# Four Q/K products moved across blocks, the sums of x in another order, and W1's last tiles split beside the MLP

## The chip, the cores and the metric

One Trainium2 chip, one of its cores. The metric is the device time of one execution in microseconds (us). Each kernel is run several times and the median counts.

## The reference, cut to what matters

The input x has 2048 tokens of 1024 features. It is normalised (xn), goes through multi-head attention with 32 heads of 32 features (s), and beside it through a two-layer MLP with the Mish activation and a SiLU behind it (g); the result is x + s * g.

```python
xn = _layernorm(x)
qkv = xn @ wqkv                                   # 1024 -> 3 x 1024, 32 heads of 32
scores = einsum("bhqd,bhkd->bhqk", q, k) * 32 ** -0.5
s = (softmax(scores) @ v) @ wo
h = xn @ w1 + b1                                  # 1024 -> 3584
act = h * tanh(softplus(h))                       # Mish
g = silu(act @ w2)                                # 3584 -> 1024
out = x + s * g
```

## The kernel before, in words

All matmuls are done with numbers split into two parts, a rounded high part (copied on ScalarE, ACT) and the remainder, the low part (a subtraction on VectorE, DVE, or on GpSimd, POOL). A full product is three matmuls: high by high, high by low, low by high (`THREE`). Split x lies in eight tiles `xc[c][half]`, for four chunks c of 512 tokens and two halves of the features. The program runs in four stages.

**Normalisation and V.** x is normalised, transposed and split, chunk by chunk, while V's first half is computed; a second pass of 16 groups (`v_group(1, t)`, the loop over i from 0 to 15) computes V's second half, 24 matmuls a group. During this second pass DVE computes sums and differences of the chunks of x (`t_half`, 16 calls, one behind each group), which the next stage needs: for the token pair of chunks 0 and 1 they go to DRAM (`ts`), for the pair 2 and 3 they overwrite chunks in place that have had their last use. One of them, `ts[4]`, goes through DRAM and comes back as `xr`. Beside this W1's first tiles are split on POOL and stored (`w1_early`, `W1_V` of the 28 tiles), and split x is stored for the MLP (`x_store`). At group 9 the raw weights of block 0 are loaded, at 11 POOL forms their sums, at 12 and 13 the first four weight pieces are split.

**Q and K.** Sixteen blocks q, of 128 columns each of Q and of K for one token pair (blocks 0 to 7 for chunks 2 and 3, 8 to 15 for chunks 0 and 1). A block computes a 2 x 2 block product with seven instead of eight smaller products, as Strassen and Winograd do; the products are named `A11, S2, A12, S3, S1, A22, S4` = 0 to 6, and a product is 12 matmuls (`product`). It needs a piece of weights (`piece`: a copy on ACT, a subtraction), sums of raw weights (`w_sum`), and one of seven tiles of x (`X`). Between the products ACT and DVE evacuate (`e0`, `e1`, `e3`, `out_`), and pieces are prepared two products ahead. Before block 8 five of the tiles of x are reloaded with those of the other token pair: `x_load` is called behind products 0 to 4 of block 7 (`NEXT`), and each of its four slices waits on SyncE's queue (SP) until PE has read the slice that it overwrites. SP's queue works in order; raw weights (`q_load`), the stores and loads of W1 half tiles (`presplit`, up to three a block, split on POOL) and `x_load` share it. From block 11 on, score matmuls of head 0 (`s_mm`) run between the products; at block 9 the tiles for them are filled with constants (`stacks`, `hl_`, `pad2`).

**The planned part.** Scores, exponentials, the product with V, the MLP's two layers and the start of the output projection run interleaved. A planner (`Plan`) writes the order of every engine out when the program is built, from costs and due times; `LEAN`, a string of digits with one for each 21 us of planned time, tilts its choices. POOL adds the exponentials up (`z`). In the first of four chunks W2 is loaded raw through one buffer (`w2r`), split (ACT, POOL) and stored; `w2` is a ring of five tiles, and W1's tiles come split from DRAM (`load_w1`).

**The end.** The rest of the output projection, SiLU, the product and the sum with x.

Of the kernel before, what the change touches and what calls it, by code (L numbers as in the profile page):

```python
# [18 lines left out]
P = 128  # L19
# [7 lines left out]
W1_V = 8  # L27
# [23 lines left out]
LEAN = ("13000510047567756073468724860620770704718277635355470747314774488"  # L51
        "67603848577224744706616776073777870776675418742527505766070872000")
# [176 lines left out]
def body(ctx: ExitStack, tc: tile.TileContext, x, wqkv, wo, w1, b1, w2, out):  # L229
# [319 lines left out]

    def piece(n, eng):  # L550
        q, i = divmod(n, 7)
# [3 lines left out]
        src = {A11: raws[q][0][:, :HK], A12: raws[q][0][:, HK:], A22: raws[q][1][:, HK:]}.get(i)  # L555
        if src is None:
            src = sums[q][i]
# [11 lines left out]
    def t_half(p, k, half):  # L569
# [3 lines left out]
        def whole(out_, c, kk):  # L573
            u = xc[c][kk][:, :, k]
            nc.vector.tensor_tensor(out_, u[:, 0].bitcast(F32), u[:, 1].bitcast(F32), ALU.add)

        def less(out_, a, b):
            nc.vector.tensor_tensor(out_, a, b, ALU.subtract)

        def split(i, src, home):  # L580
            dst = staged(f"ts{p}_{k}_{i}") if home is None else home[:, :, k]
            copy(dst[:, 0], src)
            low(nc.vector, dst[:, 1], src, dst[:, 0])
            if home is None:
                move(ts[i][:, :, k], dst)
# [9 lines left out]
        else:  # L595
            less(t[2], t[2], t[0])
            whole(t[3], c0, 1)
            less(t[3], t[2], t[3])
            split(1, t[2], None if p else xc[3][0])
            split(3 if p else 4, t[3], None)  # L600

    for i, t in enumerate([4, 5, 6, 7, 12, 13, 14, 15, 0, 1, 2, 3, 8, 9, 10, 11]):
        v_group(1, t)()
        if i % 2 == 0 and i < 10:
            w1_early()
        if i in (0, 2, 4, 6, 9, 11, 13):
            x_store()
        t_half(1 if i < 8 else 0, i % 8 // 2, i % 2)
        if i == 9:
            q_load(0, [vp.tile([P, KT, P], F32, tag="x", name=f"raw{half}", bufs=XB) for half in range(2)])  # L610
        if i == 11:
            s12 = vp.tile([P, 2, HK, P], F32, tag="x", name="s12", bufs=XB)
            s3 = vp.tile([P, 2, HK, P], F32, tag="x", name="s3", bufs=XB)
            w_sum(nc.gpsimd, 0, S1, s12[:, 0])
            w_sum(nc.gpsimd, 0, S2, s12[:, 1])
            w_sum(nc.gpsimd, 0, S3, s3[:, 0])
        if i in (12, 13):
            for n in (2 * (i - 12), 2 * (i - 12) + 1):
                piece(n, nc.gpsimd)
# [18 lines left out]
    def stacks(pool_, i):  # L638
# [3 lines left out]
        if i == 0:  # L642
            nc.gpsimd.memset(qst[i][96:P, :].bitcast(F32), 0.0)
            move(zeros, qst[i][96:P, :])
            nc.vector.memset(kst[i][96:P, :].bitcast(F32), 0.0)
# [66 lines left out]
    jobs = iter([(f, half) for f in range(W1_V, FT) for half in range(2)])  # L712
# [18 lines left out]
    def s_tile(which):  # L731
        return sp.tile([P, HK, P], F32, tag=f"ws{which}", name=f"ws{which}")

    def x_load(dst, src):
        for k in range(HK):
# [26 lines left out]
    def product(q, i, bank_, e):  # L762
        c0, c1 = PAIRS[q // KT]
        w, xx = pieces.pop(7 * q + i), X[q // KT][i]
# [3 lines left out]
        n = 0  # L768
        for k in range(HK):
            for a, b in THREE:  # L770
                nc.tensor.matmul(ps, w[:, a, k], xx[:, b, k], start=n == 0 and i in (0, 1, 4), stop=n == 3 * HK - 1,  # L771
                                 skip_group_check=i not in (0, 1, 4))
                n += 1

        def after():
            if i in (0, 1, 3):
                e[i] = sp.tile([P, 512], F32, tag=f"e{i}", name=f"e{q}_{i}")
# [22 lines left out]
    for q in range(NQ):  # L800
        bank_, e = {}, {}
        for i in range(7):
            n = 7 * q + i
            after = product(q, i, bank_, e)
            if n >= 2 and n % 2 == 0:
# [692 lines left out]
```

## Time and profile before

| | us |
|---|---|
| median of 3 runs | 3402.02 |
| lowest and highest | 3395.75, 3402.33 |
| the profiled execution | 3399.99 |
| its span in the profile | 3398.2 |
| busy: PE (matmul) | 3355.3 |
| busy: DVE, POOL, ACT | 2540.1, 2516.8, 2037.3 |

The span is what the profiler saw from the first to the last instruction; the profiled execution's own time is 1.8 us longer. Busy time is the sum over an engine's instructions. A row of the timeline gives start, duration, engine, line of the program, operation, output and inputs, and in brackets the idle time of the engine just before it and what released it. PE's matmuls are pipelined, so a row's duration holds some overlap with the next. SPq and ACTq are the queues on which SP and ACT issue DMAs.

### The profile page before, as it was taken

The page shows a single profiled execution, that of the slowest core. Times are in us where ns is not written, and L with a number is a line of the kernel's source. Part 1 is how long each engine was busy: PE and PEld are TensorE (multiplying, and loading weights), DVE is VectorE, ACT ScalarE, POOL GpSimd, SP SyncE. Part 2 cuts the span into 40 slices and gives each one's busy share as a digit, 9 for nine tenths or more (in the row PEclk, how much of TensorE's full clock was granted, in tenths as well). Part 3 has the DMA queues.
Part 4 walks back from the last instruction along what each step waited for, and adds up shares of the span by engine and source line. Part 5 has one row for each costly group of instructions (what it writes and reads, how often), then busy time and mean ns, then how long its engine had stood idle before and what let it go on. Part 6 is the DMA issues. An engine that isn't in the chain of part 4 may idle for free.

```text
span 3398.2 us, 45889 instructions
## 1 busy us (share of the span) xinstructions
PE 3355.3 (99%) x16867; PEld 2461.8 (72%) x16867; DVE 2540.1 (75%) x4020; ACT 2037.3 (60%) x3272; POOL 2516.8 (74%) x759
## 2 busy tenths in 40 slices
PE   8989899999999999999999999999999999999999
PEld 7868677677777767777677777777777767777787
DVE  6566588878788877888778877888888777886542
ACT  5333234666776667666666676666676666666621
POOL 1236454999999999888888798887888888888800
PEclk9999999999999999999999999999999999999999
DMA  6989987444344454343334533343445443333382
GB/s 206 316 303 300 305 260 237 142 128 150 119 146 136 135 165 148 101 125 106 119 102 123 185 114 114 110 127 98 128 116 182 126 118 119 106 118 118 132 302 86
DMA packets 308115, 532.75 MB, mean 157 GB/s; under 512 B 88794, under 2 KB 153306, under 8 KB 285658
## 3 DMA queue, kind: packets, MB, share of 16 engines
q1 hardware_dynamic: 288180, 488.15, 46.0%
q10 hardware_dynamic: 19712, 41.69, 3.4%
q8 instruction: 133, 2.18, 0.3%
q14 instruction: 90, 0.74, 0.1%
HBM read 379.55 MB, written 149.16 MB: 156 GB/s over the span
## 4 chain that ended last, share of the span: by engine, by line
PE 91%; DMA 3%; DVE 3%; POOL 1%; ACT 1%; issue 1%; SPq 1%; ACTq 0%; POOLq 0%; DVEq 0%
PE y L1240 18%; PE h L1150 18%; PE t L969 14%; PE s L887 13%; PE pv L1016 13%; PE op L1339 5%; PE v L351 3%; PE q_y L771 2%; PE q_x L771 2%; PE q_z L771 2%; PE zp L1042 1%; DMA w1e<-in_B_w_dram 1%; PE pt L420 0%; DMA praw<-in_B_w_dram 0%; DVE mx L677 0%
## 5 line engine op out<-in xcount | busy, mean ns | idle before, releaser
L998 POOL TENSOR_TENSOR z<-z,p 128x2048 f32<-128x2048 f32 x448 | 2067.3, 4615 | 150.0 <-ACT p L282 126.1
L282 ACT ACTIVATE p<-t,zero 128x512 f32<-128x512 f32 x2048 | 1374.5, 689 | 544.7 <-PE t L969 526.8
L893 DVE TENSOR_REDUCE mx<-s 128x1 f32<-128x512 f32 x1984 | 1325.6, 687 | 401.7 <-PE s L887 393.6
L1240 PE MATMUL y<-w,act 128*128 128x512 f32 x2688 | 928.1, 391 | 0.1
L969 PE MATMUL t<-qstack,kstack 128*128 128x512 f32 x2048 | 798.7, 392 | 1.0 <-DMA qstack<-mt 1.0
L887 PE MATMUL s<-kstack,qstack 128*128 128x512 f32 x1984 | 774.2, 393 | 3.0 <-DVE mx L893 1.5
L1150 PE MATMUL h<-xr,w 128*128 128x512 f32 x2016 | 700.3, 390 | 0.0
L1240 PEld LDWEIGHTS y<-w,act 128*128 128x128 f32 x2688 | 503.6, 188 | 112.7 <-issue 5.0
L969 PEld LDWEIGHTS t<-qstack,kstack 128*128 128x128 f32 x2048 | 383.3, 188 | 109.7 <-issue 20.9
L1016 PE MATMUL pv<-p,v 128*32 128x512 f32 x4096 | 459.3, 594 | 0.0
L887 PEld LDWEIGHTS s<-kstack,qstack 128*128 128x128 f32 x1984 | 369.9, 188 | 121.7 <-issue 23.5
L1150 PEld LDWEIGHTS h<-xr,w 128*128 128x128 f32 x2016 | 378.2, 188 | 81.3 <-issue 2.5
L1262 DVE TENSOR_TENSOR yacc<-yacc,y 128x512 f32<-128x512 f32 x416 | 283.0, 681 | 63.3 <-PE y L1240 62.4
L1016 PEld LDWEIGHTS pv<-p,v 128*32 128x32 f32 x4096 | 123.4, 110 | 283.1 <-issue 282.1
L998 POOL TENSOR_TENSOR z<-p,p 128x2048 f32<-128x2048 f32 x32 | 148.1, 4627 | 183.8 <-PE zp L1042 112.9
L1150 PE MATMUL h<-xc,w 128*128 128x512 f32 x672 | 228.2, 391 | 0.3 <-ACT p L282 0.3
L351 PE MATMUL v<-vw,xc 128*128 128x512 f32 x768 | 179.9, 393 | 0.1
L351 PEld LDWEIGHTS v<-vw,xc 128*128 128x128 f32 x768 | 143.4, 189 | 30.3 <-ACT xc L285 0.6
L1150 PEld LDWEIGHTS h<-xc,w 128*128 128x128 f32 x672 | 125.9, 188 | 26.6 <-ACT p L282 0.7
L771 PE MATMUL q_y<-xc,wq 128*128 128x512 f32 x480 | 120.5, 399 | 13.8 <-DVE e L760 5.2
L285 ACT ACTIVATE act<-h 128x512 fp32r<-128x512 f32 x112 | 66.6, 595 | 88.9 <-DVE h L1199 87.9
L771 PEld LDWEIGHTS q_y<-xc,wq 128*128 128x128 f32 x480 | 91.1, 192 | 36.7 <-DVE e L760 5.7
(139 smaller groups left out, 2947.9 us busy)
## 6 DMA issues: line engine op xcount, KB each, us to landing
w<-w1s SPq DMA_DIRECT2D x112, 1024.0 KB
w<-w2s SPq DMA_DIRECT2D x168, 512.0 KB
w2s<-w SPq DMA_DIRECT2D x56, 512.0 KB
qstack<-qs SPq DMA_DIRECT2D x96, 256.0 KB
kstack<-ks SPq DMA_DIRECT2D x96, 256.0 KB
w1s<-pw SPq DMA_DIRECT2D x40, 512.0 KB
qs<-qst ACTq DMA_DIRECT2D x32, 512.0 KB
ks<-qst ACTq DMA_DIRECT2D x32, 512.0 KB
```

The source lines that it names most:

```text
L282: nc.scalar.activation(out_, in_, fn, bias=zero if bias is None else bias, scale=scale)
L351: nc.tensor.matmul(ps, xc[t // 4][k // HK][:, a, k % HK, (t % 4) * P:(t % 4 + 1) * P], vw[i, k // 2][:, b, k % 2], start=n == 0, stop=n == ...
L771: nc.tensor.matmul(ps, w[:, a, k], xx[:, b, k], start=n == 0 and i in (0, 1, 4), stop=n == 3 * HK - 1, skip_group_check=i not in (0, 1, 4))
L887: nc.tensor.matmul(sp_, qst[h % 3][:, qt * P:(qt + 1) * P], kst[h % 3][:, kc * 512:(kc + 1) * 512], start=True, stop=True)
L893: nc.vector.reduce_max(tiles["mx"][:, qt, kc:kc + 1], tiles[qt, kc], axis=AX.X)
L969: nc.tensor.matmul(tp, kst[h % 3][:, kt * P:(kt + 1) * P], qst[h % 3][:, c * 512:(c + 1) * 512], start=True, stop=True)
L998: nc.gpsimd.tensor_tensor(zs[h], pts[T - 1] if kt == 1 else zs[h], pts[T], ALU.add)
L1016: nc.tensor.matmul(pv[h][c * DH:(c + 1) * DH, :], vt[h][:, k, :], pts[T - kt + k][:, c * 512:(c + 1) * 512], start=k == 0, stop=k == NT - 1)
L1150: nc.tensor.matmul(t["h"], w1t[n][:, a, k], xts_[c][k // HK][:, b, k % HK], start=i == 0, stop=i == 3 * KT - 1)
L1240: nc.tensor.matmul(t["y"], acts[n][:, p, s * P:(s + 1) * P], w2t[m_][:, q], start=j == 0 and i == 0, stop=j == YB - 1 and i == 2)
L1262: nc.vector.tensor_tensor(ya, ya, t["y"], ALU.add)
L1339: nc.tensor.matmul(ps[t, dh], ohl[t // 4, k][:, a, s * P:(s + 1) * P], wt[k][:, b, r], start=k == 0 and i == 0, stop=k == KT - 1 and i == 2)
```

## The change

- Products (7, 0) and (7, 2) move into block 6, behind (6, 2) and (6, 3); (8, 0) and (8, 2) into block 7, behind (7, 4) and (7, 5) (`SEQ`). The tiles of x that they release are reloaded in another assignment (`X[1]`, `NEXT`). `e0` gets a second buffer.
- The half sums of x are taken from a list, two of them behind groups 8, 10 and 12, so that all are issued by group 12. In each second half three instructions move from DVE to POOL. The raw weights of block 0 are loaded at group 5 into tiles that live on (`held`), their four sums formed at group 8, the first pieces split at groups 13 and 14 with DVE; the second load and DVE's sums at the entry to Q/K go.
- W1: 4 instead of 8 tiles are split early, 17 instead of 20 as half tiles in the Q/K stage (not in blocks 6 to 8 instead of not in 7 and 8), and the last 7 as 14 half-tile jobs in the planned part, one with each tile of h from the third on (`w1_job`), through the `w2` ring and the `w2r` buffer, split on ACT and DVE.
- W2: a raw load takes its `w2` tile at once, and every second low part moves from POOL to DVE.
- At block 9 three constant fills move from DVE to POOL; from block 11 on every second piece's low part moves from DVE to POOL; the weight sums, `q_load` and the fills are issued with the pieces instead of behind the products.
- The digits of `LEAN` are others.

```diff
-W1_V = 8
+W1_V, W1_Q, W1_JOB = 4, 21, 2
...
+    EARLY = {(6, 2): [(7, 0)], (6, 3): [(7, 2)], (7, 4): [(8, 0)], (7, 5): [(8, 2)]}
+    MOVED = [x for v in EARLY.values() for x in v]
+    SEQ = [x for q in range(NQ) for i in range(7) if (q, i) not in MOVED for x in [(q, i)] + EARLY.get((q, i), [])]
+    held = {w: big.tile([P, HK, P], F32, tag=f"ws{w}", name=f"ws{w}") for w in (S1, S3, S4)}
...
         else:
+            whole(t[3], c0, 1, nc.gpsimd)
             less(t[2], t[2], t[0])
-            whole(t[3], c0, 1)
-            less(t[3], t[2], t[3])
+            less(t[3], t[2], t[3], nc.gpsimd)
             split(1, t[2], None if p else xc[3][0])
-            split(3 if p else 4, t[3], None)
+            split(3 if p else 4, t[3], None, nc.gpsimd)
+    halves = [(p, k, half) for p in (1, 0) for k in range(HK) for half in range(2)]
     for i, t in enumerate([4, 5, 6, 7, 12, 13, 14, 15, 0, 1, 2, 3, 8, 9, 10, 11]):
         v_group(1, t)()
-        if i % 2 == 0 and i < 10:
+        if i == 0:
             w1_early()
...
-        t_half(1 if i < 8 else 0, i % 8 // 2, i % 2)
-        if i == 9:
+        if i == 5:
             q_load(0, [vp.tile([P, KT, P], F32, tag="x", name=f"raw{half}", bufs=XB) for half in range(2)])
-        if i == 11:
...
+            nc.sync.dma_start(held[S3], wqkv[HK * P:, D:D + P].rearrange("(k p) f -> p k f", p=P))
+        if i == 8:
+            s23 = vp.tile([P, 2, HK, P], F32, tag="x", name="s23", bufs=XB)
+            for which, to in ((S1, held[S1]), (S2, s23[:, 0]), (S3, s23[:, 1]), (S4, held[S4])):
+                w_sum(nc.gpsimd, 0, which, to)
+        for _ in range(2 if i in (8, 10, 12) else 1):
+            if halves:
+                t_half(*halves.pop(0))
+        if i in (13, 14):
+            for n in (2 * (i - 13), 2 * (i - 13) + 1):
+                piece(n, nc.vector)
...
-            nc.vector.memset(kst[i][96:P, :].bitcast(F32), 0.0)
+            nc.gpsimd.memset(kst[i][96:P, :].bitcast(F32), 0.0)
             nc.vector.memset(kst[i][96:98, :].bitcast(F32), 1.0)
...
-         [xc[0][0], xc[2][0], xc[0][1], xc[3][0], xc[2][1], xc[1][0], xc[1][1]])
+         [xc[0][0], xc[2][0], xc[0][1], xc[2][1], xc[3][0], xc[1][0], xc[1][1]])
-    NEXT = {0: (X[1][1], ts[1]), 1: (X[1][3], ts[2]), 2: (X[1][4], ts[0]), 3: (X[1][5], ts[3]),
+    NEXT = {0: (X[1][1], ts[1]), 2: (X[1][3], ts[2]), 1: (X[1][4], ts[0]), 3: (X[1][5], ts[3]),
...
-    q_load(0, ring_of(0))
     q_load(1, ring_of(1))
     x_load(xr, ts[4])
-    sums[0] = {}
-    for which in (S1, S2, S4):
-        w_sum(nc.vector, 0, which, s_tile(which))
...
+    for n, (q, i) in enumerate(SEQ):
+        after = product(n)
+        for m in (n + 2, n + 3) if n >= 2 and n % 2 == 0 else ():
+            piece(m, nc.vector if q < 11 or m % 2 else nc.gpsimd)
...
+        if i in (0, 2, 5) and not 5 < q < 9:
+            presplit()
...
+        own = op("SP", 0.1, emit=raw, take=["w2", "w2r"], bytes_=P * 512 * 4)
+        a = op("ACT", 0.6, need=[own], emit=lambda at: copy(t["w"][:, 0], t["raw"]))
+        a = op("DVE", 0.73, need=[a], emit=lambda at: low(nc.vector, t["w"][:, 1], t["raw"], t["w"][:, 0]), give=["w2r"])
+        w1_kept.setdefault(f, []).append(op("SP", 0.1, need=[a], emit=keep, give=[("w2", own)], bytes_=P * 1024 * 4))
...
-        a = op("SP", 0.1, emit=raw, need=need, take=["w2r"], bytes_=P * 512 * 4)
-        w2_took[m] = a = op("ACT", 0.6, need=[a], emit=high, take=["w2"])
+        w2_took[m] = a = op("SP", 0.1, emit=raw, need=need, take=["w2", "w2r"], bytes_=P * 512 * 4)
+        a = op("ACT", 0.6, need=[a], emit=high)
...
+        w2_ops[m] = a = op("DVE" if m % 2 else "POOL", 0.73 if m % 2 else 1.3, need=[a], emit=rest, give=["w2r"],
+                           key=None if m % 2 else -1)
...
+            if 0 <= n - W1_JOB < 2 * (FT - W1_Q):
+                w1_job(W1_Q + (n - W1_JOB) // 2, (n - W1_JOB) % 2)
```

More of the change, by code (lines that the diff above doesn't have):

```diff
@@ L554, in piece @@
         w = pieces[n] = pieces["tile"][:, :, n % 2 * HK:n % 2 * HK + HK]
[L555 to L557 removed]
+        if i == A22:
+            src = raws[q][1][:, HK:] if q else held[S3]
+        else:
+            src = raws[q][0][:, :HK] if i == A11 else raws[q][0][:, HK:] if i == A12 else sums[q][i]
         copy(w[:, 0], src, scale=-1.0 if i == A22 else 1.0)
@@ L710, in load_w1 @@
         move(w1t[n], w1s[n % FT])
-    jobs = iter([(f, half) for f in range(W1_V, FT) for half in range(2)])
+    jobs = iter([(f, half) for f in range(W1_V, W1_Q) for half in range(2)])
     def presplit():
@@ L731, in s_tile @@
     def s_tile(which):
-        return sp.tile([P, HK, P], F32, tag=f"ws{which}", name=f"ws{which}")
+        return (sp if which == S2 else big).tile([P, HK, P], F32, tag=f"ws{which}", name=f"ws{which}")
     def x_load(dst, src):
@@ L760, in plus, with product @@
         nc.vector.tensor_tensor(out_, a, b, ALU.add)
-    def product(q, i, bank_, e):
+    banks_, es = {}, {}
+    def product(n):
+        q, i = SEQ[n]
+        bank_, e = banks_.setdefault(q, {}), es.setdefault(q, {})
         c0, c1 = PAIRS[q // KT]
-        w, xx = pieces.pop(7 * q + i), X[q // KT][i]
+        w, xx = pieces.pop(n), X[q // KT][i]
         if i in (0, 1, 4):
```

112 lines of the change are left out of this document (53 added, 59 removed).

## The prediction

> **What bounds the kernel now.** I read the page first, then the windows, then the timeline where the windows show a hole, then who was waited for.
>
> ```profile
> span 3398.2 us, 45889 instructions
> PE 3355.3 (99%) x16867; PEld 2461.8 (72%) x16867; DVE 2540.1 (75%) x4020; ACT 2037.3 (60%) x3272; POOL 2516.8 (74%) x759
> ```
>
> TensorE (PE) is the bound, and the change removes none of its matmuls. Only time in which PE stands or runs slowly can be won or lost. The windows say where that is (span, then busy time and count of each engine, granted clock, DMA share, GB/s):
>
> ```profile
> 200.80:242.90 42.10, 30.70 (x109) 23.55 (x107) 24.09 (x31) 10.30 (x19) 14.82 (x12) 0.84 0.81 257
> 242.90:353.20 110.30, 110.10 (x484) 90.82 (x485) 74.29 (x95) 39.50 (x71) 75.56 (x61) 1.00 0.92 300
> 353.20:401.40 48.20, 40.81 (x163) 30.52 (x161) 22.46 (x32) 13.59 (x24) 10.94 (x8) 0.90 1.01 338
> 401.40:446.10 44.70, 42.70 (x171) 34.74 (x172) 28.40 (x36) 13.56 (x24) 25.03 (x19) 0.91 0.85 260
> 446.10:562.40 116.30, 113.79 (x489) 90.64 (x488) 96.67 (x149) 33.17 (x63) 51.26 (x44) 1.00 0.78 248
> 562.40:1310.00 747.60, 742.83 (x3826) 526.75 (x3825) 600.82 (x958) 521.73 (x849) 685.17 (x199) 1.00 0.47 146
> 1310.00:3219.10 1909.10, 1909.10 (x9970) 1362.30 (x9969) 1499.98 (x2360) 1280.34 (x2018) 1610.45 (x372) 1.00 0.40 122
> ```
>
> The second row is the Q/K stage undisturbed: 110.30 us for 484 matmuls, 0.228 each, so 2.73 us for a product of 12. The planned part (last two rows) has 4.8 us of idle PE in 2657, so hardly anything to win. The holes are in rows one, three and four, where the clock falls too.
>
> **Part A, the entry to Q/K (sums of x, weights of block 0).** PE in the timeline:
>
> ```profile
> 200.81 2.88 PE L771 MATMUL q_x<-xc,wq 128*128 128x512 f32 x12
> ...
> 210.48 0.49 PE L771 MATMUL q_y<-xc,wq 128*128 128x512 f32 x1 [4.75 <-ACT xc L285]
> ...
> 212.76 5.28 PE L771 MATMUL q_x<-xc,wq 128*128 128x512 f32 x12
> 223.07 5.34 PE L771 MATMUL q_y<-xc,wq 128*128 128x512 f32 x12 [5.02 <-DVE e L760]
> 228.25 2.92 PE L771 MATMUL q_z<-xc,wq 128*128 128x512 f32 x12
> 231.01 2.88 PE L771 MATMUL q_y<-xr,wq 128*128 128x512 f32 x12
> ...
> 242.97 3.04 PE L771 MATMUL q_x<-xc,wq 128*128 128x512 f32 x12 [0.92 <-ACT e L285]
> ```
>
> Four products take 228.25 - 200.81 = 27.4 us instead of 10.9, so 16.5 are lost, and 1.0 more at 242.97: 17.5. What they waited for, in the timelines of POOL, ACT, DVE and SP:
>
> ```profile
> 194.89 1.29 POOL L548 TENSOR_TENSOR s<-raw 128x512 f32<-128x512 f32 x1 [28.23 <-DMA raw<-in_A_wqkv_dram]
> 197.58 0.63 ACT L285 ACTIVATE wq<-s 128x512 fp32r<-128x512 f32 x1 [3.68 <-POOL s L548]
> 220.27 0.69 DVE L548 TENSOR_TENSOR ws<-raw 128x512 f32<-128x512 f32 x1 [7.73 <-DMA raw<-in_A_wqkv_dram]
> 213.17 5.09 SPq L540 DMA_DIRECT2D raw<-in_A_wqkv_dram  x4
> 218.31 3.69 SPq L289 DMA_DIRECT2D xr<-ts  x4
> ```
>
> First wait: ACT stands in order behind weight pieces whose sums came late, and the last sums of x stand behind it. Second: DVE stands for block 0's raw weights, loaded a second time at 213.17, with the evacuation that PE needs behind it. The change issues raw weights four V groups earlier and only once, keeps the sums in tiles that live on, and finishes all 16 half sums at group 12 of 0 to 15, three groups (about 16 us) before the entry. Both waits go. Next late is xr, needed at product 5, 200.8 + 13.7 = 214.5. SP is free for it after the last V store, about 202, then two raw issues (5.09 / 4 each) and four of xr (3.69): done about 208.5. Today xr was there at most 12.7 us after its first issue (218.31 to 231.01, no wait); from 205 that is 217.7, 3 us late at worst. Four early W1 tiles leave this stretch, whose SP and POOL they occupied; they return as jobs in the planned part (below).
>
> Against it: a third of the half sums' DVE work moves to POOL, and the two disturb each other:
>
> ```profile
> 200.54 1.78 DVE L293 TENSOR_TENSOR ts<-turned,ts 128x512 fp32r<-128x512 f32 x1
> 211.84 0.69 DVE L293 TENSOR_TENSOR ts<-turned,ts 128x512 fp32r<-128x512 f32 x1
> 200.03 1.75 POOL L293 TENSOR_TENSOR wq<-s,wq 128x512 fp32r<-128x512 f32 x1
> ```
>
> The same DVE instruction takes 1.78 beside POOL and 0.69 alone. 24 instructions of up to 1.75 on POOL are 42 us of overlap at most; at a loss of 1.09 in 1.78 that holds DVE up 26 us over the whole stage, where it does 24 x 0.69 = 17 less: 9 us net at worst, inside the 16 of lead. The Trainium skill, "GPSIMD Engine Reference", section 1 (Specifications), says GpSimd's SBUF interfaces are shared with VectorE, with contention for DVE instructions with two SBUF inputs; the three rows agree. By that rule moving work to POOL gains nothing for DVE, and A would be worth what the lead leaves: this is a rival below. I leave 2 of the 17.5 (bounds 0 and 9): **-15.5**.
>
> **Part B, the change of token pairs.** Today five chunk halves are reloaded as products of blocks 7 and 8 release them:
>
> ```profile
> 352.30 2.88 PE L771 MATMUL q_x<-xc,wq 128*128 128x512 f32 x12
> ...
> 385.63 0.93 PE L771 MATMUL q_y<-xc,wq 128*128 128x512 f32 x3
> 387.85 0.98 PE L771 MATMUL q_y<-xc,wq 128*128 128x512 f32 x3 [1.29 <-DMA xc<-ts]
> ...
> 396.21 2.90 PE L771 MATMUL q_z<-xc,wq 128*128 128x512 f32 x6 [3.48 <-DMA xc<-xs]
> ...
> 406.86 2.90 PE L771 MATMUL q_y<-xc,wq 128*128 128x512 f32 x12
> ```
>
> 385.63 to 406.86 is 21.2 us for three products of 2.73, so 13.0 are lost: some 11 of late data and 2 of slow clock. The DMA view of 353.2 to 401.4:
>
> ```profile
> DMA packets 10929, 16.28 MB, mean 338 GB/s; under 512 B 494, under 2 KB 3820, under 8 KB 10927
> ...
> xc<-ts SPq DMA_DIRECT2D x16, 512.0 KB
> ```
>
> Twenty slices of 512 KB are 10.5 MB of the 16.3, and the DMA share was 1.01: bandwidth, not order, is the limit. With (7,0) after (6,2), the first release comes 4 products or 10.9 us earlier; the last use, (8,6), keeps its place. More must now pass: a second pair of raw tiles (1.05 MB) and two more Q/K stores (1.05), less one W1 store (0.5): 1.6 MB, 4.7 us at 338. The data is 11 - 10.9 + 4.7 = about 4.8 late; the W1 half-tile jobs dropped in block 6 take some off. I leave 4.5 (bounds 0 and 9): **-8.5**. Moving the products adds no work: a second buffer for e0 only.
>
> **Part C, the fills at block 9.**
>
> ```profile
> 411.13 1.81 POOL L643 MEMSET qstack<- 32x2048 f32 x1
> 417.64 1.76 DVE L645 MEMSET kstack<- 32x2048 f32 x1 [0.48 <-issue]
> 422.65 4.58 PE L771 MATMUL q_z<-xc,wq 128*128 128x512 f32 x12 [2.00 <-DVE e L760]
> ```
>
> Two such fills hold DVE, and PE loses 2.00 and 4.58 - 2.88 = 1.7 of slow clock: 3.7. One fill goes to POOL, but the other (of ones, over it) then waits on DVE for POOL, which has two sums and the 1.81 fill ahead; behind it in DVE's queue stand a piece and (9,3)'s evacuation, for which (9,5) waits. By my count that arrives between 0 and 4 us late; I take 1: **-2.7**. On the slow clock the Trainium skill, "TensorE: Matmul & The Clock Gate", part 1, says it halves after an idle window of about 3.4 us. Here a wait of 2.00 was enough, so the row decides; by the page C would be worth 1.7 less.
>
> **Part D, blocks 11 to 15.** Every second piece's low part goes from DVE (busy 96.67 of 116.30) to POOL (51.26). PE idles 2.5 there. Bounds -2.5 to +3 (pieces stuck behind POOL's jobs); I take **-0.7**.
>
> **Part E, the planned part.** New leanings reorder the same matmuls: the orders show 96 changes into column mode in both. W1's last 7 tiles come as 14 half jobs through W2's single raw buffer; half of W2's low parts move from POOL to DVE. SP's issues into that buffer, and W1's loads:
>
> ```profile
> 721.66 0.43 SPq L1105 DMA_DIRECT2D w2r<-in_B_w_dram  x1
> 735.63 0.55 SPq L1105 DMA_DIRECT2D w2r<-in_B_w_dram  x1
> 741.95 0.56 SPq L1105 DMA_DIRECT2D w2r<-in_B_w_dram  x1
> 756.77 0.55 SPq L1105 DMA_DIRECT2D w2r<-in_B_w_dram  x1
> L289 SPq DMA_DIRECT2D w<-w1s x112: 319/344/779, 557.1 to 3172.0; - x112
> ```
>
> A use of the buffer takes 14.0, 6.3 and 14.8 us (long behind POOL's z sums); a tile of h has (3172.0 - 557.1) / 111 = 23.6. New per tile: one half behind POOL 14.4, one on DVE 6.3, one W1 job 6.3: 27, over 23.6 for 14 tiles, but before and behind them there is slack of 2.9 a tile. Other streams cover it, as the 4.8 us of idle PE suggest. Bounds -3 and +9; I take **+0.6**.
>
> **Sum:** -15.5 - 8.5 - 2.7 - 0.7 + 0.6 = -26.8. The profiled execution took 3399.99 (3398.2 and 1.8 around it), 2.0 under the median of 3402.02: 3373.2 + 2.0 = **3375**.
>
> **Rivals.** (1) Bandwidth keeps B: the loads start earlier but finish where they did, since blocks 6 and 7 already fill the queues (0.92 of share in row two). B gains 1.5 instead of 8.5: 3382. (2) DVE and POOL slow each other so that the last sums of x still miss the entry: A keeps 9: 3382. (3) Slower: the raw buffer. 14 tiles x 3.4 us = 48 us of W2 lateness, if the five W2 tiles ahead and the attention streams don't cover it: 3375 + 48 = 3423. It decides from some 27 us uncovered on; against it, today's chain refills the buffer without a pause (741.95, 756.77) and PE does not wait for it. (4) The new order of the planned part loses what Q/K wins: 3402.
>
> **Chances:** forecast 0.62, (1) 0.14, (2) 0.11, (3) 0.06, (4) 0.07. A measurement can tell about 0.2%, 6.8 us. Faster: 0.62 + 0.14 + 0.11 less 0.01 for overlap of (1), (2) and bad bounds: 0.86; same 0.07; slower 0.07. Range: best bounds of A, B and C alone give 3375 - 2 - 4.5 - 1 - 3 = 3364, all to the good 3360; (1) and (2) together, with D's bound, give 3393. So 3361 to 3394.
>
> **What would show it.** Right: PE's first eight products after the V stage without a gap over 1 us and at clock 1.00; the loads xc<-ts starting 11 us earlier relative to block 8; raw weights loaded once. Wrong: a wait of q_y on xr, of q_z on xc<-xs as long as 3.48, a DVE fill waiting on POOL at block 9, waits of y on w2, or a planned part over 2836 us.

## The result, and the profile after

| | before | after |
|---|---|---|
| median of 4 runs, us | 3401.35 | 3456.51 |
| lowest and highest | 3395.75, 3402.33 | 3451.74, 3461.32 |
| the profiled execution, its span | 3399.99, 3398.2 | 3455.92, 3454.1 |
| first score of the planned part starts (end of Q/K) | 562.36 | 550.08 |
| from there to the end of the span | 2835.8 | 2904.0 |

The changed kernel is slower by 1.7%: the ratio to before is 1.0166, interval 1.0148 to 1.0184. The spans differ by 55.9 us. Q/K ended 12.3 us earlier and the rest took 68.2 us longer.

From the page of after:

```profile
span 3454.1 us, 45962 instructions
PE 3375.7 (98%) x16867; PEld 2469.0 (71%) x16867; DVE 2634.9 (76%) x4023; ACT 2049.4 (59%) x3286; POOL 2510.2 (73%) x740
```

From its windows, with the columns of the windows shown of before:

```profile
550.10:1310.00 759.90, 713.40 (x3544) 495.41 (x3546) 659.20 (x929) 493.49 (x798) 615.01 (x160) 0.98 0.48 147
1310.00:3219.10 1909.10, 1909.10 (x9969) 1362.94 (x9961) 1504.87 (x2385) 1281.47 (x2023) 1604.87 (x372) 1.00 0.41 123
```

The same number of matmuls, but the first stretch of the planned part got through 3544 in 760 us, where before got through 3826 in 748. From there to 3219 us hardly anything differs. In the first stretch DVE is busy 58 us more. PE stands 46.5 us in it (759.90 less 713.40), where before it stood 4.8. That is 42 of the 68 us; some 26 are left for matmuls that took longer, 201 ns of busy PE each on average against 194 (713.40 / 3544 and 742.83 / 3826), at a granted clock of 0.98 instead of 1.00. Whom PE waited for in that stretch of after (total, times, longest; the first three rows):

```profile
PE t L976 <- DVE mx L900: 14.6, 9, 3.4
PE s L894 <- DVE mx L900: 12.9, 8, 2.9
PE s L894 <- DVE yacc L1290: 3.7, 2, 2.3
```

Two rows more for the maxima, of 3.7 and 2.8, make it 34.0 us for them. Before, the largest row of this list was 1.5 us in all (`PE s`, for the same maxima). Where DVE's time went, from the groups of instructions (count, busy us, mean ns of one):

```profile
L900 DVE TENSOR_REDUCE mx<-s 128x1 f32<-128x512 f32 x556 | 366.4, 684 | 63.3 <-PE s L894 61.1
L293 DVE TENSOR_TENSOR w<-w2r,w 128x512 fp32r<-128x512 f32 x28 | 64.5, 2304 | 7.7 <-ACT w L285 7.6
L293 DVE TENSOR_TENSOR w1w<-w1r,w1w 128x512 fp32r<-128x512 f32 x14 | 43.8, 3128 | 5.5 <-ACT w1w L285 5.5
L1227 DVE TENSOR_TENSOR h<-h,r 128x512 f32<-128x512 f32 x28 | 19.4, 693 | 0.3
```

The second and third rows are the 42 low parts that the change put on DVE. They take 2.30 and 3.13 us, though the same subtraction takes 0.69 where POOL is idle. The fourth row is a multiplication of the same size, one of whose inputs (`h`) lies in PSUM: 0.693. The 42 are the only DVE instructions of this size in the stretch with both inputs in SBUF. Of the 108 us of the 42, 42 x 0.69 = 29 are their own work; 79 are not. What a long one waits for is seen in the timelines of DVE, POOL and PE side by side:

```profile
611.04 2.99 DVE L293 TENSOR_TENSOR w1w<-w1r,w1w 128x512 fp32r<-128x512 f32 x1
613.96 6.55 DVE L900 TENSOR_REDUCE mx<-s 128x1 f32<-128x512 f32 x10
608.88 4.60 POOL L1005 TENSOR_TENSOR z<-z,p 128x2048 f32<-128x2048 f32 x1
613.55 4.93 POOL L1005 TENSOR_TENSOR z<-z,p 128x2048 f32<-128x2048 f32 x1
614.69 0.50 PE L976 MATMUL t<-qstack,kstack 128*128 128x512 f32 x1 [1.57 <-DVE mx L900]
```

The low part is issued at 611.04, while POOL is in the middle of a sum of 4.60 us. It ends at 614.03, which is 0.55 after the end of POOL's sum (608.88 + 4.60 = 613.48), about its own length of 0.69. Ten maxima stand behind it, and PE waits 1.57 for one of them. The Trainium skill, "SBUF — State Buffer", section "Who interferes with whom", has this rule: a DVE instruction with two SBUF inputs and a GpSimd instruction that reads SBUF exclude each other for the whole instruction. The trace agrees with it here, 2.99 against 0.69.

In the Q/K stage, PE's timeline of after at the sites of A (first three rows), B (two), C (two) and D:

```profile
204.55 4.70 PE L784 MATMUL q_x<-xc,wq 128*128 128x512 f32 x12 [3.96 <-ACT wq L285]
223.36 0.97 PE L784 MATMUL q_y<-xr,wq 128*128 128x512 f32 x3 [1.18 <-DMA xr<-ts]
237.78 2.88 PE L784 MATMUL q_z<-xc,wq 128*128 128x512 f32 x12
350.33 2.97 PE L784 MATMUL q_y<-xc,wq 128*128 128x512 f32 x12 [0.88 <-DVE e L769]
373.12 5.46 PE L784 MATMUL q_y<-xc,wq 128*128 128x512 f32 x12 [3.50 <-issue]
402.42 4.58 PE L784 MATMUL q_y<-xc,wq 128*128 128x512 f32 x12 [1.91 <-DVE e L769]
409.58 2.88 PE L784 MATMUL q_x<-xc,wq 128*128 128x512 f32 x12
435.19 0.70 PE L682 MATMUL s<-kstack,qstack 128*128 128x512 f32 x2 [3.69 <-DMA w1s<-pw]
```

The fifth row names no releaser for its 3.50; DVE's evacuation of that bank ran from 372.33 to 373.01, right ahead of it. The third row is product 4 of block 1, which before started at 248.94: A won 11.2. The seventh is the start of block 10, before at 427.07: 17.5 won so far, so B and C together 6.3. By the first score of the planned part 12.3 were left: blocks 10 to 15 lost 5.2. Six of the runs below have the same V and Q/K stages; in their profiled executions Q/K ended at 551.58 to 555.42, and in one with those of before at 559.92. So these executions put what Q/K won at 4.5 to 12.3 us, and differences of a few us in its end say little.

### The profile page after: what moved, and what is told of

The parts are those of the page before. It is cut to its first block, busy times and chain, and to the rows that moved or that the text cites. A ratio compares the mean times of both kernels' runs of the same rounds, so it can differ in the third digit from the quotient of the medians.

```text
span 3454.1 us, 45962 instructions
## 1 busy us (share of the span) xinstructions
PE 3375.7 (98%) x16867; PEld 2469.0 (71%) x16867; DVE 2634.9 (76%) x4023; ACT 2049.4 (59%) x3286; POOL 2510.2 (73%) x740
## 4 chain that ended last, share of the span: by engine, by line
PE 85%; DVE 8%; DMA 3%; ACT 2%; issue 1%; POOL 0%; SPq 0%; ACTq 0%; DVEq 0%; POOLq 0%
PE y L1268 17%; PE h L1178 16%; PE t L976 13%; PE s L894 12%; PE pv L1023 12%; PE op L1367 5%; PE v L351 3%; PE q_y L784 2%; DVE w L293 2%; DVE mx L900 2%; PE q_x L784 1%; PE q_z L784 1%; DVE w1w L293 1%; PE zp L1049 1%; ACT p L282 1%
## 5 line engine op out<-in xcount | busy, mean ns | idle before, releaser
L894 PE MATMUL s<-kstack,qstack 128*128 128x512 f32 x1984 | 779.3, 396 | 17.5 <-DVE mx L900 12.9
L1178 PE MATMUL h<-xc,w 128*128 128x512 f32 x672 | 238.5, 402 | 3.1 <-DVE mx L900 2.8
```

The lines of the kernel that those rows point to most:

```text
L894: nc.tensor.matmul(sp_, qst[h % 3][:, qt * P:(qt + 1) * P], kst[h % 3][:, kc * 512:(kc + 1) * 512], start=True, stop=True)
L1178: nc.tensor.matmul(t["h"], w1t[n][:, a, k], xts_[c][k // HK][:, b, k % HK], start=i == 0, stop=i == 3 * KT - 1)
```

## The experiments

All times are medians; each ratio is to runs of the kernel before on the same chip, with its interval. "Planned part" is the span less the start of the first score behind Q/K.

### What costs 68 us in the planned part

**The low parts taken off DVE and POOL.** Theory H is that held DVE instructions cost the time; the rival O is that the W1 jobs, the raw buffer and the order do.

```diff
-a = op("DVE", 0.73, ..., emit=lambda at: low(nc.vector, t["w"][:, 1], t["raw"], t["w"][:, 0]), ...)
+a = op("DVE", 0.73, ..., emit=lambda at: copy(t["w"][:, 1], t["w"][:, 0].bitcast(F32), scale=0.001), ...)
...   (and the same for the odd tiles of W2)
```

> The changed kernel with its plan kept; the 42 low parts in question are neither on DVE nor on POOL but written by ACT as a thousandth of the high part (this part of the result is left out). DVE then has no instruction with two SBUF inputs in the planned part. Theory H (the held DVE instructions cost the 68 us): PE's waits for DVE's maxima go from some 31 us to under 6, the planned part from 2904 to 2838-2860 us, the time to 3390-3412. Rival O (the 14 W1 jobs, the raw buffer and the order cost the time by themselves): the planned part stays above 2880, the time above 3432.

Measured: 3388.84, ratio 0.9970 (0.9957 to 0.9983). Q/K ends at 552.42 and the planned part takes 2832.5. Whom PE waited for from there to 1310 (the largest two rows):

```profile
PE t L976 <- ACT p L282: 0.6, 2, 0.4
PE t L976 <- DMA qstack<-mt: 0.5, 2, 0.3
```

The window:

```profile
552.40:1310.00 757.60, 755.41 (x3907) 534.48 (x3906) 613.14 (x969) 558.88 (x917) 662.27 (x173) 1.00 0.53 161
```

The jobs, the digits and every other instruction's place are those of after, and the whole loss is gone (2904.0 less 2832.5 is 71.5), with no wait for the maxima left on the list. The kernel leaves the true low parts out. Its raw buffer also comes free sooner, since for these 42 only ACT's first copy reads it; the next run has that too and keeps 50 of the 68 us, so the buffer isn't the cause. O falls. The plain work of 29 us leaves DVE too in this run, but it is less than half of the 71.5; the next three runs change the holding in other ways.

**One SBUF input instead of two.** The 42 become a multiplication of the high part by a constant, still on DVE (`nc.vector.tensor_scalar(w[:, 1], w[:, 0], 0.001, ...)`); the true low parts are left out here too.

> The changed kernel with its plan and the place of every instruction kept. The 42 low parts that it put on DVE in the planned part (14 of W1, 28 of W2) are no longer a subtraction of two SBUF tiles but a thousandth of the high part, an instruction with one SBUF input: this part of the result is left out. Theory H (a DVE instruction with two SBUF inputs is held until POOL lets go, and the maxima behind it stand): these 42 take 0.7 us or less each instead of 2.3 and 3.1 mean, PE's waits for DVE's maxima fall from some 31 us to under 8, and the planned part from 2904 us to 2845-2870, the time to 3398-3422. Rival O (the order itself, the 14 W1 jobs and the raw buffer cost the time): the 42 become short, the planned part stays at 2885 or more, the time at 3437 or more. Rival P (any DVE instruction is held beside POOL, whatever its inputs): the 42 stay at 2 us or more each, and the time within 8 us of 3456.

Measured: 3443.98, ratio 1.0130 (1.0113 to 1.0146); planned part 2886.2. The two groups, in answers on their lines (shortest, median and longest ns):

```profile
L1138 DVE TENSOR_SCALAR w<-w x28: 408/1984/4687, 574.8 to 1281.4; 128x512 fp32r<-128x512 f32 x28
L1109 DVE TENSOR_SCALAR w1w<-w1w x14: 427/2948/4450, 612.9 to 967.9; 128x512 fp32r<-128x512 f32 x14
```

H in my wording, held because of two inputs, missed: with one input they are held as before, up to 4.69 us, and only their own part shrank, from 0.69 to 0.41 (42 x 0.28 = 11.8 us; the planned part fell by 17.8). From the run above it differs by 53.7 us (2886.2 less 2832.5), of which DVE's plain work can be 42 x 0.41 = 17 at most; the rest goes with the holding. But 0.41 alone shows that this is a faster form of the instruction, so the run doesn't show that any DVE instruction is held, and the row of `h<-h,r` above, 0.693 in 28, says that it isn't so. The same section of the Trainium skill's "SBUF — State Buffer" names DVE's 2-port modes beside the two SBUF inputs as what excludes GpSimd; that fits both rows.

**W2's part alone.** The kernel before with W2's split of after (28 low parts on DVE, the raw load taking its `w2` tile at once, no W1 jobs), planned anew with the digits of before. The edit in its main lines:

```diff
-        w2_ops[m] = a = op("POOL", 1.3, need=[a], emit=rest, give=["w2r"], key=-1)
+        w2_ops[m] = a = op("DVE" if m % 2 else "POOL", 0.73 if m % 2 else 1.3, need=[a], emit=rest, give=["w2r"],
+                           key=None if m % 2 else -1)
```

> The kernel before with one part of the change alone: W2's raw load takes its ring tile at once and every second low part (28 of 56) goes from POOL to DVE, planned with the digits of the kernel before. Theory H: the 28 take over 2 us each on DVE, some 40 us more of DVE time, and the planned part goes from 2836 us to 2860-2890, the time to 3424-3454. Rival O (the W1 jobs cost the time, not DVE's low parts): the planned part stays within 10 us of 2836, the time within 10 us of 3400.

Measured: 3441.75, ratio 1.0121 (1.0106 to 1.0136); planned part 2876.4, as H had it.

```profile
L293 DVE TENSOR_TENSOR w<-w2r,w 128x512 fp32r<-128x512 f32 x28 | 69.8, 2492 | 7.6 <-ACT w L285 7.2 <-POOL z L998 0.3
```

The largest row of PE's waits in that stage (total, times, longest):

```profile
PE s L887 <- DVE mx L893: 14.5, 9, 3.2
```

With 28 held instructions 40.6 us are lost, with 42 of them 68.2: 1.45 and 1.62 each. It takes neither the W1 jobs nor the new digits to lose them.

**POOL's sums in quarters.** After, with each addition of exponentials as four instructions of 512 columns.

> The changed kernel with each z sum of 2048 columns on POOL issued as four of 512; the plan and every engine's order stay. H expects DVE's lows to last at most 0.69 + 1.3 = 2.0 us instead of up to 4.9, on average 1.2 to 1.4 instead of 2.3 (W2) and 3.1 (W1), half to two thirds of the 68 us of the planned part to come back, and a time of 3410 to 3425, if POOL itself, with some 0.5 us more for each z, does not become late. Rival S (shared bandwidth: both engines run slower side by side, whatever the length of an instruction) expects the same 2.3 and 3.1 us and 3456 or more. O and B expect no change.

Measured: 3526.18, ratio 1.0370 (1.0346 to 1.0394); planned part 2974.9. H expected means of 1.2 to 1.4 us. In the median the low parts did get shorter, from 2.25 and 3.20 us in after to 1.31 and 1.38, but a few were held so long that the means rose. Their groups, and behind them the shortest, median and longest ns of each:

```profile
L293 DVE TENSOR_TENSOR w<-w2r,w 128x512 fp32r<-128x512 f32 x28 | 87.5, 3126 | 10.5 <-ACT w L285 10.3
L293 DVE TENSOR_TENSOR w1w<-w1r,w1w 128x512 fp32r<-128x512 f32 x14 | 68.4, 4888 | 7.7 <-ACT w1w L285 5.6 <-POOL hl L293 2.2
L293 DVE TENSOR_TENSOR w<-w2r,w x28: 680/1309/13509, 576.4 to 1354.0; 128x512 fp32r<-128x512 f32 x28
L293 DVE TENSOR_TENSOR w1w<-w1r,w1w x14: 681/1378/17236, 629.5 to 1018.8; 128x512 fp32r<-128x512 f32 x14
```

One of the long ones and POOL's queue, in the timeline:

```profile
597.13 12.49 DVE L293 TENSOR_TENSOR w<-w2r,w 128x512 fp32r<-128x512 f32 x1
589.31 19.76 POOL L1007 TENSOR_TENSOR z<-z,p 128x512 f32<-128x512 f32 x16
```

The low part of 597.13 ended at 609.62, when POOL's run of sixteen ended (609.07), and not at one of the ends between them. Others in this run got in after 1.0 and 1.5 us, both (629.46 and 636.94) in the middle of another run of sixteen. So shorter instructions on POOL shortened most of the holds and made a few several times longer. What decides which stays open. More holding (156 us in the two groups instead of 108) went with more waiting for the maxima (77.5 us instead of 34.0) and a larger loss again, 71 us more. Four quarters of 1.31 us also keep POOL longer than one sum of 4.6, so not all of the 71 need be the holding.

**The low parts on POOL**, at the same places of the plan (`low(nc.gpsimd, ...)` for all 42).

> The changed kernel with one edit: the 42 low parts of the planned part that the change gave to DVE (28 of W2, 14 of W1) are issued to POOL at the same place of the written order; the plan is otherwise the same, digit for digit. Theory H (held): a DVE instruction with two SBUF inputs stands until the instruction that POOL has in hand is done (z, 4.6 us), everything behind it on DVE stands too, and that is the whole loss. H expects the planned part, 2904 us in the changed kernel and 2836 in the one before, to come back to 2836 to 2860 and the time to 3389 to 3412. Rival O (order): the new digits and the new order make the loss; it expects 3440 to 3460. Rival B (buffer): W2's raw buffer is too slow for 14 more half tiles; with all lows behind z on POOL it expects more than 3456.

Measured: 3433.22, ratio 1.0094 (1.0077 to 1.0111); planned part 2878.2. The time lies in no theory's range. PE's waits for the maxima fell to 0.7, but only 26 of the 68 us came back: PE now waits for exponentials. On ACT, which computes them, the waits for raw loads have grown to 57.2 us for W2 and 24.7 for W1, from 9.4 and 16.5 in after; the one raw buffer now comes free only when POOL, behind its sums, gets to the low part. That this is the whole rest isn't shown.

```profile
PE t L976 <- ACT p L282: 10.8, 8, 3.0
PE s L894 <- ACT p L282: 5.4, 3, 2.0
```

**The same, with the planner told** (1.3 us each on POOL).

```diff
-a = op("DVE", 0.73, need=[a], emit=lambda at: low(nc.vector, ...), give=["w2r"])
+a = op("POOL", 1.3, need=[a], emit=lambda at: low(nc.gpsimd, ...), give=["w2r"], key=-1)
```

> The changed kernel with the 42 low parts on POOL, and planned so (1.3 us each on POOL, as the other 28), with its own digits. On POOL without the planner's knowledge the planned part was 2878 us. If those remaining 42 us were the plan's ignorance of POOL's load, the planned part comes to 2840-2855 and the time to 3392-3408. If they were POOL's load itself (18 us of W1 low parts and 36 of W2's, with the sums of the exponentials behind them), it stays at 2865-2885, the time at 3418-3437.

Measured: 3465.24, ratio 1.0194 (1.0177 to 1.0211); planned part 2908.0. Neither case came. PE hardly waits for anything (the largest row of its list is 3.9 us in all), but between 800 and 1100 us the scores take 461 ns in this group, where those of the run with the low parts on ACT take 393:

```profile
L894 PE MATMUL s<-kstack,qstack 128*128 128x512 f32 x193 | 86.6, 461 | 6.2 <-DVE r L1223 2.6 <-DVE mx L900 1.4
```

The same group of the run with the low parts on ACT:

```profile
L894 PE MATMUL s<-kstack,qstack 128*128 128x512 f32 x230 | 89.7, 393 | 0.0
```

The planner wrote another order, under digits that were made for a different one. In places it has scores in a row: between 918 and 926 us they go at the pace of DVE's maxima, 11 of them in 7.09 us. How much of the loss is this order and how much POOL's load the run can't tell, so what POOL's load alone costs stays open.

**The old digits.** After with the digits of before.

> The changed kernel with the 130 digits of the plan's leanings of the kernel before. H expects the same loss in another order: DVE lows of 2 to 3 us on average, 3435 to 3470. O, as far as the digits are meant, expects the time to fall to about 3390 to 3400.

Measured: 3483.70, ratio 1.0243 (1.0228 to 1.0258); planned part 2929.5. The low parts take 2.49 and 3.10 us in the mean, as H had it, but the time is 14 us over H's range. The new digits are not the loss; they are worth 25 us to this plan. A plan and its digits belong together, which also warns of reading the run before this one as the price of an edit.

### Where Q/K's 27 us went

**Q/K's changes alone.** V and Q/K of after, with W1 as before (8 tiles early, 20 in Q/K) and the planned part of before.

> The V and Q/K stages of the changed kernel (moved products, order of the half sums, fills and pieces), with W1 split as before (8 tiles early, 20 as half tiles in the Q/K stage) and the planned part of the kernel before, its digits too. The changed kernel reaches the planned part 12.3 us earlier than the one before. H, O and B all put the loss in the planned part and expect 3389 (3384 to 3397) here, a little less gain than 12.3 if the W1 tiles slow the V stage. A loss that the Q/K changes carry over into the planned part (rival Q) would show as 3402 or more.

Measured: 3410.95, ratio 1.0033 (1.0020 to 1.0046). The time lies where Q expected it, but nothing is carried over into the planned part, which takes 2838.0, as before: Q/K begins 19 us late and ends at 574.45.

```profile
198.37 1.30 POOL L584 TENSOR_TENSOR turned<-turned 128x512 f32<-128x512 f32 x1 [4.02 <-DVE turned L584]
219.81 4.86 PE L784 MATMUL q_x<-xc,wq 128*128 128x512 f32 x12 [18.91 <-ACT wq L285]
```

POOL waits 4 us for DVE in each pair of half sums, and a pair takes some 9.2 us (POOL's subtraction starts at 189.05, 198.37, 207.62, 216.83). DVE is busy for most of that time, with instructions that take longer beside POOL's (a subtraction 1.66 us, at 193.25). After has the same chain (182.93, 192.25, 201.57), but it ends 15.3 us earlier; the run has four more W1 tiles in POOL's queue ahead of it.

**Three corrections in Q/K**, planned part untouched.

```diff
-            whole(t[3], c0, 1, nc.gpsimd)
+            whole(t[3], c0, 1)
...   (less and split of the second half sum likewise on DVE)
-    EARLY = {(6, 2): [(7, 0)], (6, 3): [(7, 2)], (7, 4): [(8, 0)], (7, 5): [(8, 2)]}
+    EARLY = {(6, 2): [(7, 0)], (6, 3): [(7, 2)], (7, 1): [(8, 0)]}
...
-            nc.vector.memset(kst[i][96:98, :].bitcast(F32), 1.0)
+            nc.gpsimd.memset(kst[i][96:98, :].bitcast(F32), 1.0)
```

> The changed kernel, planned part untouched, with three edits before it: the half sums' instructions on POOL go back to DVE; (8, 0) stands between (7, 1) and (7, 3) and (8, 2) stays in its block, so that no two products behind one another use bank y of one block; and the fill of ones at block 9 goes to POOL too. My theory of what was left at the three sites (DVE and POOL wait for one another in the half sums; two products in one bank in succession leave the evacuation no time; DVE's fill waits for POOL's): A leaves 2 instead of 7, B 3 instead of 7, C 1 instead of 4, so the last evacuation of Q/K ends at 537-543 us instead of 550, and the time is 3443-3450, since the planned part stays at 2904. If the rests have other causes (late data, the clock), Q/K ends at 547 or later and the time stays within 4 us of 3456.

Measured: 3450.86, ratio 1.0150 (1.0135 to 1.0165); planned part 2903.1. PE's timeline:

```profile
201.12 2.88 PE L784 MATMUL q_x<-xc,wq 128*128 128x512 f32 x12
218.28 0.96 PE L784 MATMUL q_y<-xr,wq 128*128 128x512 f32 x3 [1.21 <-DMA xr<-ts]
232.70 2.88 PE L784 MATMUL q_z<-xc,wq 128*128 128x512 f32 x12
375.80 3.87 PE L784 MATMUL q_z<-xc,wq 128*128 128x512 f32 x9 [2.20 <-DVE e L769]
399.85 2.88 PE L784 MATMUL q_x<-xc,wq 128*128 128x512 f32 x12
```

PE's longest wait between 110 and 560 us:

```profile
PE s L682 <- DMA w1s<-pw: 5.5, 1, 5.5
```

A: product 4 of block 1 starts at 232.70, 16.2 us ahead of before. A pair of half sums now takes 8.0 us (174.43 to 182.40, 190.38 and 198.35) instead of 9.3, though DVE has three instructions more in it: a subtraction that took 1.66 us beside POOL in after (196.44) takes 0.69 here (192.31). Block 10 starts at 399.85, 27.2 ahead; so B and C are worth 11.0. The causes named for A and C hold (C's products run without a hole); at B 2.20 are still lost. But Q/K ends at 545.38, only 17.0 ahead, and the time is 0.9 over the range that was expected. The first scores of head 0 wait 5.5 us. The list names a W1 store as the releaser; what these scores read is head 0's tiles, whose loads are on the same queue. In three runs with after's Q/K stage the list names that load itself (`DMA kstack<-ks`, 4.7), and a later run bears it out.

**The same with the planned part of before**, and 7 W1 tiles early.

> The Q/K stage of the changed kernel with the three edits of the run above, and the planned part, W2's split and the digits of the kernel before. W1: 7 tiles split before Q/K (three of them behind groups 1 to 3), 42 half tiles in the Q/K stage, none in the planned part. If the loss lies in the planned part's split alone and the Q/K gain is real, Q/K ends at 537-550 us, the planned part takes 2836-2840, and the time is 3374-3390, faster than both kernels. If seven early W1 tiles push the sums of x past the entry, as eight did when their half sums were partly on POOL, PE waits 5 to 18 us at the entry and the time is 3395-3410.

Measured: 3408.43, ratio 1.0022 (1.0012 to 1.0032). Q/K ends at 567.56 and the planned part takes 2842.8. The second case: three more early tiles make the entry late, by one wait. Head 0's load costs 5.7 us here too.

```profile
211.91 5.00 PE L784 MATMUL q_x<-xc,wq 128*128 128x512 f32 x12 [11.06 <-ACT wq L285]
```

**W1's last tiles in the Q/K stage**: 4 tiles early, 48 half tiles in Q/K (four a block from block 10 on), head 0 loaded behind block 9, low parts of pieces on DVE; planned part of before.

> The mended Q/K stage with 4 early W1 tiles, the other 24 as 48 half tiles in the Q/K stage (three a block in blocks 0 to 6 and 9, four a block from block 10 on, where the DMA share was 0.78), head 0 loaded three products after block 9's fills instead of in block 10, pieces' low parts all on DVE, and the planned part, W2's split and the digits of the kernel before. If the loss of the changed kernel lies in the planned part's DVE low parts and the rests at Q/K are those that I named, PE enters Q/K without a hole over 1.5 us, Q/K ends at 538-546 us, the planned part takes 2835-2842, and the time is 3374-3386. If head 0's load or the four half tiles a block collide from block 10 on, Q/K ends at 547-556 and the time is 3386-3396.

Measured: 3396.71, ratio 0.9995 (0.9986 to 1.0005). Q/K ends at 549.92, 12.4 ahead, without a wait for head 0; the planned part takes 2845.4, 9.6 more than before. SyncE's queue at the end of Q/K:

```profile
544.89 13.44 SPq L289 DMA_DIRECT2D w1s<-pw  x3
```

PE's waits behind it:

```profile
PE t L976 <- DMA qstack<-mt: 6.8, 2, 5.8
PE h L1177 <- DMA w<-w1s: 2.9, 1, 2.9
```

Three last stores wait for POOL on a queue that works in order, and the maxima of head 0 stand behind them (issued at 561.19). The W1 tile of the second row does not: it was issued at 544.30, ahead of them, and took 9.06 us to land.

**The half tiles spread** (four a block in blocks 1 to 3 and 10 to 14), with the change's low parts on POOL from block 11 on.

> As the run with 48 half tiles in the Q/K stage, but these spread otherwise: four a block in blocks 1 to 3 and 10 to 14, one in block 15, three in the others but 7 and 8, so that the last are stored before the planned part begins; and every second piece's low part on POOL from block 11 on, as in the changed kernel. That run ended its products some 12 us earlier than the kernel before and lost as much at the start of the planned part, where PE waited 5.8 us for the maxima's DMA and 2.9 us for a W1 tile behind late W1 stores. If the stores of block 15's jobs were the cause, these waits go and the planned part takes 2834-2840 us: 3382-3390. If W1's 48 half tiles hold the queues up wherever they stand, the time stays at 3393-3400.

Measured: 3401.80, ratio 1.0006 (0.9997 to 1.0015). The planned part takes 2841.9, not 2834 to 2840: the wait for the maxima is down to 1.0, but PE waits 5.5 for a W1 tile that stands behind three stores again. Q/K ends at 559.23, 9.3 later than in the run above; one wait for POOL has most of that, at the first block whose pieces go there beside four jobs:

```profile
449.91 4.64 PE L784 MATMUL q_y<-xc,wq 128*128 128x512 f32 x10 [7.07 <-POOL wq L293]
```

**Ended earlier, and a fifth tile early.** The two runs differ in one tile, split early or as two half tiles in Q/K (`W1_V` 4 and 5); pieces are on DVE again, the last job stands at block 15.

> As the first run with 48 half tiles in the Q/K stage, pieces' low parts on DVE as there, but the jobs end earlier: four a block in blocks 0, 3, 5 and 10 to 14, none but 7 and 8 with less than three, the last at block 15's third product. In that first run SyncE's queue stood 13.4 us behind three last W1 stores at the end of Q/K, and the planned part lost some 10 us to what was queued behind them. If that was all, Q/K ends at 549-554 us and the planned part takes 2833-2838: 3384-3392. If the 24 half tiles more per half of the stage cost as much elsewhere (queues, evacuation behind stores), 3393-3401.

> The same with a fifth W1 tile split before Q/K (behind group 1) and 46 half tiles in the Q/K stage (four a block in blocks 0 and 10 to 14). If one early tile more still leaves the sums of x in time, it is 0 to 4 us faster than the run beside it. If each early tile of the three more that cost 11 us at the entry costs its third, PE waits 3-4 us at the entry, and the time is level or up to 4 us longer.

Measured: 3395.02, ratio 0.9986 (0.9977 to 0.9996), and 3397.05, ratio 0.9991 (0.9983 to 1.0000). The planned part is back at 2836.9 and 2836.4, but Q/K ends at 561.07 and 562.65, as before. (The profiled executions were 4.7 and 3.9 us slower than the medians, so some of that may be chance.) The two times can't be told apart. In the first, blocks 2 to 4 now wait for evacuations on ACT (the longest of 3.15 us), block 8 for data again:

```profile
291.44 4.31 PE L784 MATMUL q_x<-xc,wq 128*128 128x512 f32 x12 [3.15 <-ACT e L285]
394.22 2.90 PE L784 MATMUL q_z<-xc,wq 128*128 128x512 f32 x6 [1.78 <-DMA xc<-xs]
```

In the second the entry waits:

```profile
205.51 4.61 PE L784 MATMUL q_x<-xc,wq 128*128 128x512 f32 x12 [4.16 <-ACT wq L285]
```

So wherever I put W1's tiles back into Q/K, the gain went: each of the last four runs is within 0.2% of before. That no other place would do isn't shown. No full version that I ran beats the kernel before by more than that. That the seven tiles could be split in the planned part without loss is shown only by the run that leaves their low parts out.

## Why the prediction was wrong, step by step

It gave 3375, range 3361 to 3394, and the chances 0.86 to faster; 3456.5 was measured. (Its lower end comes out as 3362 by its own bounds, not 3360; nothing hangs on that.) Its sum, with what each term measured:

| term | predicted | measured in after | with the causes removed |
|---|---|---|---|
| A, entry | -15.5 | -11.2 | -16.2 |
| B and C | -8.5 and -2.7 | -6.3 | -11.0 |
| D, blocks 11 to 15 | -0.7 | +5.2 | not reached alone |
| E, planned part | +0.6 | +68.2 | -3.3 (low parts off DVE) |

**E is the step that failed.** "Half of W2's low parts move from POOL to DVE" was costed only through the raw buffer, as 6.3 us a use; the instruction on DVE was never priced, and the bounds of -3 to +9 had no row for it. The row stood in the prediction itself, in part A: 1.78 beside POOL, 0.69 alone, with the Trainium skill's rule on shared interfaces. There the neighbours on POOL last 1.3 to 1.8 us. In the planned part they last 4.6, POOL is busy in nine tenths of that stretch, and the maxima that release PE stand behind on DVE. The runs show in its place 42 instructions of 2.30 and 3.13 us, 34.0 us of PE's waits for the maxima, and a planned part 68.2 us longer. A bound from rows at hand was there: 42 x up to 4.6 = 193 us on DVE, and DVE had 601 of 748 us busy. "4.8 us of idle PE in 2657, so hardly anything to win" was right, and it also says that there was no slack to lose anything into: a stage in which PE never waits is one where every engine arrives just in time.

**A:** the wait for the second load of raw weights went, and the size is within the bounds (7 us of some 18 are left, bounds 0 and 9). What it had wrong is the lead. It took all half sums to be done three groups, 16 us, before the entry, because they are issued by group 12; but DVE runs behind, and even with POOL out of the half sums the last one ends at 199.0, 2 us before the entry. In after ACT has the last one (202.86) ahead of the weight piece (203.88) for which PE waits 3.96. So the 9 us net at worst for DVE and POOL slowing each other had nothing to cover them: a pair took 9.3 us with POOL and 8.0 without. xr came 1.2 late, as "3 us late at worst" allowed.

**B and C:** the sizes hold when their own new waits are removed (11.0 against 11.2). The prediction counted the data that would be late (none is in after) and said that moving the products adds no work. It didn't ask what stands next to what: products 1 and 3 of a block use one PSUM bank, and without product 2 between them PE waits for the evacuation of the first. C's wait on POOL was named, at 0 to 4 us, and came: PE lost 3.6 there (1.91 and a product of 4.58 instead of 2.88).

**D:** nothing in the prediction stood for head 0's load. Its last piece was issued at 428.07, 17.8 us earlier than before (445.91), in step with block 10; but the first score came 7.1 us behind that issue instead of 4.1, at a DMA share of 1.03 and 1.01 from 425 to 435 us, where before had 0.96 and 0.91 from 440 to 450. With the load put behind block 9 its wait went, while the half tiles' other costs stayed. The wait grew from 1.02 to 3.69; the other half of the 5.2 us stays open.

**The rivals:** (1) did not come: no late tile of x at the change of pairs is on after's list. (2) came, with 7 of its 9 us. (4) had the right place, but not the cause, since the same order without the 42 loses nothing, and less than half the size (27 us, where 68 were lost). (3) did not: no wait of y for a W2 tile is on after's list. The sign to look for, "a planned part over 2836 us", was the right one.

## What to carry to other kernels

An instruction moved to another engine must be priced by rows of the stage it goes to, beside the neighbours that it will have there, and with what stands behind it in its new queue; a rule read in one part of a change has to be put to every other part. In a stage where the bound engine never idles, take any new instruction on an in-order queue ahead of its releasers as a loss until a row bounds it. And when a change makes room in one stage by moving work out, ask first where that work can stand at all: here its place decided more than the room.

## What the runs showed of the hardware that I had not expected

A subtraction of two SBUF tiles on DVE lasted 2.30 and 3.13 us in the mean beside POOL's sums of 4.6 us, up to 4.92, against 0.69. An instruction with one SBUF input, 0.41 us alone, was held just as long (up to 4.69), while a multiplication with one input in PSUM was not (0.693). Cutting POOL's sums into quarters of 1.31 us brought the medians down to 1.31 and 1.38 but the means up to 3.13 and 4.89, with 12.49 in the row shown, which ended where POOL's run of sixteen ended. I had taken a shorter neighbour for a cure.
